# Attention and a feed-forward layer on one core: 20 of 24 joined pairs have their softmax weights turned by VectorE in 32x32 blocks and placed by DMAs through device memory

## The chip, the cores and the metric

The kernel runs on one core of a Trainium2 chip. A core has five engines that run beside one another: TensorE (PE: matmuls; PEld are its weight loads), VectorE (DVE), ScalarE (ACT), GpSimd (POOL) and SyncE (SP), which here only issues DMAs. The metric is the device time of one execution in microseconds (us).

## The reference: what is computed

A batch of 8 with 8 heads, 576 tokens and 64 channels goes through two attentions, whose sum `x` goes through a gated layer of two products:

```python
q_d, k_d, v_d = means of 4 neighbouring tokens        # 144 pooled tokens
out_up    = repeat(softmax(q_d k_d^T / 8) v_d, 4)
out_local = softmax(q k^T / 8 where |i - j| < 4) v     # a band of 7 keys
x   = (out_up + out_local)                             # 4608 tokens x 512 channels
h   = x @ w_in                                         # 2048 hidden channels
out = where(h >= 1, h, where(h <= -1, 0, (h + 1)**2 / 4)) @ w_out
```

## The kernel before

**Two streams on TensorE.** Attention is done a pair of heads at a time; there are 8 x 4 = 32 pairs. The first 8 (`SECOND = 8`) are done in an opening part of their own. The other 24 are done one at a time by the generator `join`, between the steps of the feed-forward layer. The layer is worked through in chunks of 384 tokens; a step `n` is 12 matmuls of the first product (`mm1`, tile `ffn_h`, L858) and 9 of the second (`mm2`, tile `ffn_o`, L921), the second product belonging to an earlier step. `JOINS` lists by hand the steps at which the 24 pairs begin; its last entry is a closing call that only finishes the last pair. `tc.keep_in_program_order` (`put`) fixes the order of all of a join's matmuls on TensorE, so a matmul that waits holds up everything behind it there.

**One join.** The call `join(n)` at step J first issues, on TensorE, the value products of the pair before: `value_ps<-ap,vd` (L633) is the very first of its matmuls, then come the scores of pair n (`score_ps`, L651 and L619) and the local value products `value_ps<-al,v` (L675). During the next step VectorE, GpSimd and ScalarE make the softmax: `sl` holds the local weights (5 pairs of windows of 64 tokens, 128x640), `sp` the pooled ones (128 x 3 x 144). VectorE normalises `sl` at L746 and `sp` at L247 and L254.

**The turn.** The value products need the weights turned, keys on partitions. Before, TensorE does it. For pairs 10 and later (`moved`, 22 of the 24), SP copies `sl` and `sp` to `local` and `pooled` in on-chip memory, which gives the words the type that a one-pass transpose takes (L759, L761, L762). At step J + 2, after that step's `mm2`, TensorE does 5 transposes into `local_ps` (L776) and 6 into `turn_ps` (L779). ScalarE then copies them to `ap` (L784) and `al` (L789), where the next join finds them.

**The DMA queue.** Nearly all DMAs go out from SP in one order; a DMA that waits for its data holds up all that stand behind it. Besides the join's own (`q_sb`, `k_sb`, `v`, `vq_sb` for the next pair) these are the results (`out<-osb`) and sums of weights kept in device memory for the end (`kept<-words`).

Of the kernel before, what the change touches and what calls it, by code (L numbers as in the profile page):

```python
# [10 lines left out]
F32 = mybir.dt.float32  # L11
# [35 lines left out]
WIN = 64  # L47
WIN_START = [0, 58, 116, 174, 232, 285, 343, 401, 459, 512]
OUT_START = [0, 61, 119, 177, 235, 288, 346, 404, 462, 520]
OUT_LEN = [61, 58, 58, 58, 53, 58, 58, 58, 58, 56]  # L50
NB = len(WIN_START)
NG = NB // 2

# [25 lines left out]
QB = 48  # L79
NQB = SD // QB  # L80
# [66 lines left out]
SECOND = 2 * NPAIR  # L147
NALL = B * NPAIR
JOINS = [17, 20, 23, 26, 30, 37, 44, 51, 58, 63, 68, 73, 78, 85, 92, 99, 106, 111, 115, 120, 125]
JOINS += [131, 135, 138, 142]  # L150
assert len(JOINS) == NALL - SECOND + 1


class Rotation:
# [10 lines left out]
def attention_then_ffn(ctx: ExitStack, tc, qT, kT, vw, vp, vq, members, w_in, w_out, out):  # L165
# [431 lines left out]
    def pooled_sums(n):  # L597

        pooled_sum("q")
        pooled_sum("k")  # L600

    def join(n, pool):

        scores = pool.tile([P, 2, 512], F32, name="score_ps", tag="ga")
# [10 lines left out]
        def pooled_scores(i):  # L615
            for h in range(2):
                hs = slice(h * D, (h + 1) * D)
                x = h if i < 2 else 1 - h
                put(nc.tensor.matmul(  # L619
                    sp_v[i][x * D : (x + 1) * D, :],  # L620
                    state["qd"][hs, i * QB : i * QB + D],
                    state["kd"][hs, :],
                    start=True,
                    stop=True,
                    skip_group_check=True,
                ))

        def pooled_values(main):
            ap, vd = state["ap"], state["vd"]
            for h in range(2):  # L630
                hs = slice(h * D, (h + 1) * D)
                ks = slice(0, P) if main else slice((1 - h) * D, (2 - h) * D)
                put(nc.tensor.matmul(  # L633
                    pp_v[hs, :],
                    vd[ks, hs] if main else vd[ks, P : P + D],
                    ap[ks, 0 if main else 1, :, h, :],
                    start=main,
                    stop=not main,
                    skip_group_check=True,
                ))  # L640
# [3 lines left out]
        if n < NALL:  # L644
            q, k = loaded["q"], loaded["k"]
            for g in range(NG):
                for h, s in ((0, 0), (1, 1), (1, 0), (0, 1)):
                    x = h ^ s
                    w = WIN_START[x * NG + g]
                    hs = slice(h * D, (h + 1) * D)  # L650
                    put(nc.tensor.matmul(  # L651
                        sl_v[x * WIN : (x + 1) * WIN, s, g * WIN : (g + 1) * WIN],
                        q[hs, w : w + WIN],
                        k[hs, w : w + WIN],
                        start=True,
                        stop=True,
                        skip_group_check=True,
                    ))
            pooled_scores(0)
        if n > SECOND:  # L660
            pooled_values(False)
        if n < NALL:
            pooled_scores(2)
            pooled_scores(1)
        if n > SECOND:
# [47 lines left out]
        if n > SECOND:  # L713
            x = apool.tile([P, S], F32, name="x", tag="ap", bufs=1)
            xd = apool.tile([P, SD], F32, name="xd", tag="kd", bufs=1)
            nc.vector.tensor_scalar_mul(xd, pp_v, 1.0 / FACTOR)
# [29 lines left out]
        nc.vector.tensor_tensor(  # L746
            slf, slf, scales[:, 0:NB].unsqueeze(2).broadcast_to([P, NB, WIN]), op=ALU.mult
        )
        normalised = normalise(sp, scales)
        vpt = loaded["vp"]  # L750
        vd = apool.tile([P, P + D], F32, name="vd", tag="vd", bufs=1)
        state["vd"] = vd
        with tc.issue_after(shifted.ins):
            nc.gpsimd.tensor_tensor(vpt[:, 0:2, :], vpt[:, 0:2, :], vpt[:, 2:4, :], op=ALU.add)
            nc.gpsimd.tensor_tensor(vd, vpt[:, 0, :], vpt[:, 1, :], op=ALU.add)
        moved = n > SECOND + 1
        if moved:
            local = apool.tile([P, NG * P], F32, name="local", tag="al", bufs=1)
# [559 lines left out]
```

## Time and profile before

| | us |
|---|---|
| median of three runs (lowest to highest) | 889.43 (888.37 to 890.03) |
| the profiled execution: its own time | 889.52 |
| the profiled execution: its span | 887.7 |

| engine | busy us | share of the span |
|---|---|---|
| TensorE matmuls | 876.8 | 99% |
| VectorE | 554.5 | 62% |
| ScalarE | 460.0 | 52% |
| GpSimd | 369.9 | 42% |

The span is what the trace covers, from its first instruction to its last; 1.8 us of the execution's time lie around it. The times in all rows count from the start of the span. The profiled execution stands 0.09 us above the median of the runs. A row of the timeline gives the start, the time that the row covers, the engine, the line, the operation and the tiles; an "x5" merges five neighbouring instructions into one row.

### The profile page before, as it was taken

Reading aid. Unit: us, or ns where it says so; the run is one execution under the profiler, and the core shown is the slowest. Engines: PE = TensorE matmul, PEld = TensorE weight load, DVE = VectorE, ACT = ScalarE, POOL = GpSimd, SP = SyncE. Lnnn points to the kernel's source line nnn. Section 1 sums busy time; section 2 is a strip of 40 time slices with the busy share of each in tenths; the row PEclk is TensorE's granted clock in tenths of the full one; section 3 lists DMA queues with packets and bytes.
Section 4 is the critical chain, followed back from the end, with each engine's and each line's share of the span. In section 5 each row is a group of like instructions: output and inputs, shape, how many; then the busy total and the mean of one; then the engine's idle time right before and its main releaser. Section 6 shows DMA issues by size and latency. Waiting matters only on the chain. (4 is left out here: it accounts for less than half of the span.)

```text
span 887.7 us, 19656 instructions
## 1 busy us (share of the span) xinstructions
PE 876.8 (99%) x7766; PEld 793.7 (89%) x7766; DVE 554.5 (62%) x1062; ACT 460.0 (52%) x1015; POOL 369.9 (42%) x365
## 2 busy tenths in 40 slices
PE   8999999999999999999999999999999999999998
PEld 6788888999999899999999998999999989999997
DVE  7999884775566556566666566665546557744452
ACT  5788864555545545545544544454455544434333
POOL 4366664454334424444433343444334435433232
PEclk9999999999999999999999999999999999999999
DMA  9685113343323423333333233342233222334341
GB/s 351 236 294 198 43 55 126 89 139 106 106 89 103 134 78 106 128 117 116 129 100 106 91 113 99 108 161 93 86 104 99 93 84 75 116 95 143 117 119 51
DMA packets 68172, 106.44 MB, mean 120 GB/s; under 512 B 5712, under 2 KB 34128, under 8 KB 68080
## 3 DMA queue, kind: packets, MB, share of 16 engines
q1 hardware_dynamic: 67648, 104.76, 36.2%
q8 instruction: 61, 1.00, 0.5%
q10 hardware_dynamic: 432, 0.43, 0.1%
q14 instruction: 31, 0.25, 0.1%
HBM read 71.48 MB, written 17.83 MB: 101 GB/s over the span
## 5 line engine op out<-in xcount | busy, mean ns | idle before, releaser
L902 POOL TENSOR_TENSOR gl<-u,gh 128x384 fp32r<-128x384 f32 (+1 forms) x176 | 193.5, 1100 | 395.6 <-ACT gh L896 308.8
L921 PE MATMUL ffn_o<-w_o,gh 128*128 128x512 f32 x1152 | 346.1, 382 | 0.0
L858 PE MATMUL ffn_h<-xh,w_i 128*128 128x384 f32 (+1 forms) x1184 | 301.3, 337 | 0.4 <-ACT m L879 0.2
L921 PEld LDWEIGHTS ffn_o<-w_o,gh 128*128 128x128 f32 x1152 | 211.2, 189 | 24.5 <-issue 0.2
L858 PEld LDWEIGHTS ffn_h<-xh,w_i 128*128 128x128 f32 x1184 | 209.5, 189 | 16.2 <-ACT m L879 4.2
L921 PE MATMUL ffn_o<-w_o,gl 128*128 128x512 f32 x576 | 218.3, 379 | 0.0
L858 PE MATMUL ffn_h<-xl,w_i 128*128 128x384 f32 (+1 forms) x592 | 197.2, 333 | 0.0
L883 DVE TENSOR_SCALAR u<-m 128x384 f32<-128x384 f32 (+1 forms) x160 | 77.4, 483 | 141.2 <-ACT m L879 127.9
L889 DVE SCALAR_TENSOR_TENSOR u<-m,u 128x384 f32<-128x384 f32 (+1 forms) x160 | 107.8, 674 | 79.5 <-ACT u L886 79.5
L896 ACT CAST gh<-u 128x384 fp32r<-128x384 f32 (+1 forms) x176 | 95.5, 542 | 116.2 <-DVE u L889 115.7
L886 ACT ACTIVATE u<-u 128x384 f32<-128x384 f32 (+1 forms) x176 | 97.2, 552 | 111.0 <-DVE u L883 110.6
L921 PEld LDWEIGHTS ffn_o<-w_o,gl 128*128 128x128 f32 x576 | 108.9, 189 | 15.5
L858 PEld LDWEIGHTS ffn_h<-xl,w_i 128*128 128x128 f32 x592 | 111.9, 189 | 2.2
L879 ACT COPY m<-ffn_h 128x384 f32<-128x384 f32 (+1 forms) x132 | 63.8, 484 | 55.8 <-PE ffn_h L858 50.3
L728 ACT ACTIVATE sl<-sl 128x640 f32<-128x640 f32 x24 | 17.8, 740 | 55.5 <-POOL sl L702 55.5
L582 POOL TENSOR_TENSOR xl<-x,xh 128x576 fp32r<-128x576 f32 (+4 forms) x32 | 35.4, 1112 | 16.6 <-ACT xh L581 16.6
L959 DVE SCALAR_TENSOR_TENSOR sums<-sums 128x128 f32<-128x128 f32 (+1 forms) x72 | 33.1, 460 | 1.8
L702 POOL TENSOR_TENSOR sl<-sl,mxl 128x640 f32<-128x640 f32 x24 | 30.3, 1262 | 1.7 <-DVE mxl L701 1.6
L837 POOL TENSOR_TENSOR w_i<-m,w_i 128x512 fp32r<-128x512 f32 x16 | 22.0, 1380 | 21.5 <-ACT w_i L832 21.5
L1078 POOL TENSOR_TENSOR m<-both 128x256 f32<-128x256 f32 x14 | 10.2, 730 | 45.5 <-DVE both L1077 40.9
L837 POOL TENSOR_TENSOR w_o<-m,w_o 128x512 fp32r<-128x512 f32 x16 | 21.8, 1367 | 13.5 <-ACT w_o L832 13.5
L1071 DVE TENSOR_TENSOR both<-ffn_h,both 128x256 f32<-128x256 f32 x14 | 5.9, 424 | 33.9 <-PE ffn_h L1052 29.4
(180 smaller groups left out, 1159.5 us busy)
## 6 DMA issues: line engine op xcount, KB each, us to landing
xh<-kept SPq DMA_DIRECT2D x56, 256.0 KB, 3.7
v<-vw SPq DMA_DIRECT2D x29, 320.0 KB, 4.0
vq_sb<-vq SPq DMA_DIRECT2D x24, 384.0 KB, 3.2
out<-osb SPq DMA_DIRECT2D x35, 256.0 KB, 2.4
raw_o<-w_out SPq DMA_DIRECT2D x16, 512.0 KB, 7.2
raw_i<-w_in SPq DMA_DIRECT2D x16, 512.0 KB, 7.7
kept<-words SPq DMA_DIRECT2D x32, 256.0 KB, 2.6
k_sb<-kT SPq DMA_DIRECT2D x28, 288.0 KB, 4.3
```

What stands on the lines that cost most here:

```text
L582: nc.gpsimd.tensor_tensor(xl[:, p, dst], x[:, part], xh[:, p, dst], op=ALU.subtract)
L702: shifted = nc.gpsimd.tensor_tensor(slf, slf, ml.unsqueeze(2).broadcast_to([P, NB, WIN]), op=ALU.subtract)
L837: engine.tensor_tensor(w[:, 1], raw[name, f, "m"], w[:, 0], op=ALU.subtract)
L858: ins = nc.tensor.matmul(htiles[c, f], wi[:, wt, cc * P : (cc + 1) * P], turns(xt[:, cc, ts]), start=(cc == 0 and xt is xh and wt == 0), s ...
L879: utiles["copied"] = nc.scalar.copy(m, h)
L883: nc.vector.tensor_scalar(utiles[c, f], m if c > 0 else h, -1.0, 1.0, op0=ALU.max, op1=ALU.add)
L886: nc.scalar.activation(u, u, AF.Square, scale=0.5)
L889: utiles["last"] = nc.vector.scalar_tensor_tensor(u, utiles["m"] if c > 0 else h, 1.0, u, op0=ALU.max, op1=ALU.min)
L896: nc.scalar.copy(gh, utiles[c, f])
L902: nc.gpsimd.tensor_tensor(gl, utiles.pop((c, f)), gh, op=ALU.subtract)
L921: ins = nc.tensor.matmul(o, gt[:, ts], turns(weights["o", f][:, wt, :]), start=f == 0 and n == 0, stop=f == NFC - 1 and n == 2,)
L959: return nc.vector.scalar_tensor_tensor(out, a, 1.0, b, op0=ALU.mult, op1=op)
```

## The change

A set `TURNED` holds those pairs, from the third joined pair on, after which at least four steps follow before the next join. By the list `JOINS` these are 20 pairs: 4 of them with four steps to the next join (those that start at steps 26, 111, 131 and 138), 7 with five, 1 with six, 8 with seven. For them:

```diff
+TURN_START = WIN_START[: NG - 1] + [S // 2 - 61] + WIN_START[NG:]
+TURN_PARTS = [[(0, 32, 2)]] + [[(3, 29, 2)]] * (NB - 2) + [[(8, 24, 1), (32, 32, 1)]]
+TURNED = {SECOND + i for i in range(2, NALL - SECOND) if JOINS[i + 1] - JOINS[i] >= 4}
...
+    def turn(n, sl, sp):
+        al = apool.tile([P, NG * P], F32, name="al", tag="al", bufs=1)
+        ap = apool.tile([P, 3, 160], F32, name="ap", tag="ap", bufs=1)
+        nc.vector.transpose(
+            al.rearrange("p (b x c) -> p b x c", b=2, c=32), sl.rearrange("p g r (b c) -> p b (g r) c", c=32)
+        )
+        flat = sl.rearrange("p g r c -> p (g r c)")[:, 0:480].rearrange("p (k i c) -> p k i c", k=5, c=32)
+        nc.vector.transpose(flat[:, 0:4], sp[:, :, 0:P].rearrange("p i (k c) -> p k i c", c=32))
+        nc.vector.transpose(flat[:, 4], sp[:, :, SD - 32 : SD])
+        local = dram.tile([P, NG * P], F32, name="local", tag="local", bufs=2)
+        pooled = dram.tile([160, 2, 160], F32, name="pooled", tag="pooled", bufs=2)
+        for x in range(2):
+            for a in range(2):
+                rows = slice(x * WIN + a * 32, x * WIN + a * 32 + 32)
+                nc.sync.dma_start(
+                    local[x * WIN : (x + 1) * WIN, a * 320 : (a + 1) * 320].rearrange("(b c) f -> c b f", b=2),
+                    al[rows].rearrange("c (b f) -> c b f", b=2),
+                )
+        nc.sync.dma_start(al, local)
+        for x in range(2):
+            for a in range(2):
+                rows = slice(x * WIN + a * 32, x * WIN + a * 32 + 32)
+                nc.sync.dma_start(
+                    pooled[:, x, a * WIN : (a + 1) * WIN].rearrange("(k c) f -> c k f", k=5),
+                    flat[rows, :, 0:2].rearrange("c k i f -> c k (i f)"),
+                )
+            nc.sync.dma_start(
+                pooled[:, 1 - x, P:].rearrange("(k c) f -> c k f", k=5), flat[rows, :, 2],
+            )
+        nc.sync.dma_start(ap[:, 0:2], pooled[0:P])
+        for h in range(2):
+            nc.sync.dma_start(ap[(1 - h) * WIN : (2 - h) * WIN, 2], pooled[160 - WIN : 160, h])
+        state.update(al=al, ap=ap)
...
-                    ap[ks, 0 if main else 1, :, h, :],
+                    ap[ks, h if main else 2, 0:SD] if n - 1 in TURNED else ap[ks, 0 if main else 1, :, h, :],
...
+                    for c0, size, count in TURN_PARTS[i]:
+                        o = TURN_START[i] + c0 - r * S // 2
+                        put(nc.tensor.matmul(
+                            pl_v[hs, r, o : o + size * count],
+                            v[rs, 2 * g + h, :],
+                            turned_part(al, rs, 2 * g + r, c0, size, count),
...
-        normalised = normalise(sp, scales)
+        if n in TURNED:
+            every = scales[:, NB:].unsqueeze(2).broadcast_to([P, NQB, SD])
+            normalised = nc.vector.tensor_tensor(sp, sp, every, op=ALU.mult)
+        else:
+            normalised = normalise(sp, scales)
...
+        if n in TURNED:
+            turn(n, sl, sp)
+            yield
+            load(n + 1, "vp")
...
+            return
```

VectorE turns the 32x32 blocks of `sl` and `sp` where they lie. Four DMAs write the turned local blocks to device memory (`local`) and one reads them back in place (`al`). Six DMAs write the pooled blocks (`pooled`) and three read them back (`ap`). The 11 transposes and the two copies by ScalarE fall away, and with them the three copies by SP. A turned pair's windows are cut a little differently: its local value products are 22 instead of 20, and the scaling of the pooled result (`xd`) is done in two instructions instead of one.

**TensorE, two steps after the join at step 131**, one of the pairs with four steps to the next join. `ffn_o` and `ffn_h` are the second and the first product of the layer. Before:

```order
L921 MATMUL ffn_o_1913<-w_o_752,gl 128x512
L921 MATMUL ffn_o_1921<-w_o_752,gh 128x512 x2
L921 MATMUL ffn_o_1921<-w_o_752,gl 128x512
L776 MATMUL local_ps<-units,local 128x128 x5
L779 MATMUL turn_ps<-units,pooled 128x128 x6
L858 MATMUL ffn_h_1917<-xh,w_i_972 128x384 x2
L858 MATMUL ffn_h_1917<-xl,w_i_972 128x384
```

Now, at the same place:

```order
L1003 MATMUL ffn_o_1913<-w_o_752,gl 128x512
L1003 MATMUL ffn_o_1921<-w_o_752,gh 128x512 x2
L1003 MATMUL ffn_o_1921<-w_o_752,gl 128x512
L940 MATMUL ffn_h_1917<-xh,w_i_972 128x384 x2
L940 MATMUL ffn_h_1917<-xl,w_i_972 128x384
```

The 11 transposes are gone and nothing has come in their place.

**VectorE, the same pair, from the normalising of its weights on.** `u` belongs to the gate of the layer, `first_qd` and `kd` are the pooled sums for the next pair. Before:

```order
L746 TENSOR_TENSOR sl<-sl,score_ps 128x640
L247 TENSOR_TENSOR sp_rest<-sp,score_ps 128x6x16
L254 TENSOR_TENSOR sp<-sp,score_ps 128x3x128
L883 TENSOR_SCALAR u<-m 128x384
L593 TENSOR_REDUCE first_qd<-q_sb 128x144
L889 SCALAR_TENSOR_TENSOR u<-m,u 128x384
L593 TENSOR_REDUCE kd<-k_sb 128x144
```

Now:

```order
L816 TENSOR_TENSOR sl<-sl,score_ps 128x640
L821 TENSOR_TENSOR sp<-sp,score_ps 128x432
L965 TENSOR_SCALAR u<-m 128x384
L616 STREAM_TRANSPOSE al<-sl 128x640
L971 SCALAR_TENSOR_TENSOR u<-m,u 128x384
L620 STREAM_TRANSPOSE sl<-sp 128x384
L621 STREAM_TRANSPOSE sl<-sp 128x96
L598 TENSOR_REDUCE first_qd<-q_sb 128x144
L598 TENSOR_REDUCE kd<-k_sb 128x144
```

The first turn stands behind `u` of a layer step, the other two behind the second half of that gate, and the pooled sums of the next pair behind all three.

**SP's queue, the same pair**, from its own turn to the loads that the next join issues. Before:

```order
L759 DMA local<-sl 128x640
L761 DMA pooled<-sp 128x3x128
L762 DMA pooled<-sp_rest 128x384
L209 DMA vq_sb<-vq 128x768
L203 DMA q_sb<-qT 128x576
```

Now:

```order
L214 DMA vq_sb<-vq 128x768
L627 DMA local<-al 32x2x320 x4
L635 DMA pooled<-sl 32x5x64 x2
L631 DMA al<-local 128x640
L639 DMA pooled<-sl 32x5x32
L635 DMA pooled<-sl 32x5x64 x2
L639 DMA pooled<-sl 32x5x32
L644 DMA ap<-pooled 64x160
L642 DMA ap<-pooled 128x320
L644 DMA ap<-pooled 64x160
L208 DMA q_sb<-qT 128x576
```

Three DMAs have become 14, two of them (`al` and the first `ap`) reading what DMAs of the same pair wrote; the load of `vq_sb` has moved ahead of them.

## Rows read from the trace of the kernel before

**Rows 1.** The page, parts 1 and 2: busy time, and the granted clock in 40 slices.

```profile
PE 876.8 (99%) x7766; PEld 793.7 (89%) x7766; DVE 554.5 (62%) x1062; ACT 460.0 (52%) x1015; POOL 369.9 (42%) x365
...
PEclk9999999999999999999999999999999999999999
```

**Rows 2.** Groups by line and shape, TensorE: count | busy us, mean ns | idle.

```profile
L779 PE MATMUL turn_ps<-units,pooled 128*128 128x128 f32 x132 | 14.9, 250 | 0.0
L776 PE MATMUL local_ps<-units,local 128*128 128x128 f32 x110 | 12.0, 241 | 0.0
```

**Rows 3.** Timeline of TensorE around the transposes of the pair of step 131.

```profile
670.98 0.38 PE L921 MATMUL ffn_o<-w_o,gl 128*128 128x512 f32 x1
671.20 0.55 PE L776 MATMUL local_ps<-units,local 128*128 128x128 f32 x5
671.58 0.68 PE L779 MATMUL turn_ps<-units,pooled 128*128 128x128 f32 x6
672.09 0.56 PE L858 MATMUL ffn_h<-xh,w_i 128*128 128x384 f32 x2
672.49 0.33 PE L858 MATMUL ffn_h<-xl,w_i 128*128 128x384 f32 x1
```

**Rows 4.** Timeline of TensorE at the next join, step 135.

```profile
677.52 0.49 PE L858 MATMUL ffn_h<-xh,w_i 128*128 128x384 f32 x2
677.84 0.33 PE L858 MATMUL ffn_h<-xl,w_i 128*128 128x384 f32 x1
678.10 0.47 PE L633 MATMUL value_ps<-ap,vd 128*64 128x144 f32 x4
...
679.62 0.76 PE L675 MATMUL value_ps<-al,v 64*64 64x61 f32 x40
680.30 0.70 PE L921 MATMUL ffn_o<-w_o,gh 128*128 128x512 f32 x2
```

**Rows 5.** Timeline of VectorE, the pair of step 131.

```profile
666.64 0.82 DVE L746 TENSOR_TENSOR sl<-sl,score_ps 128x640 f32<-128x640 f32 x1
...
667.54 0.55 DVE L254 TENSOR_TENSOR sp<-sp,score_ps 128x384 f32<-128x384 f32 x1
668.01 0.38 DVE L883 TENSOR_SCALAR u<-m 128x384 f32<-128x384 f32 x1
```

**Rows 6.** Timeline of SP's issues, steps 131 to 135.

```profile
667.49 0.51 SPq L759 DMA_DIRECT2D local<-sl  x1
668.23 0.63 SPq L761 DMA_DIRECT2D pooled<-sp  x1
668.90 0.65 SPq L762 DMA_DIRECT2D pooled<-sp_rest  x1
...
679.37 0.33 SPq L203 DMA_DIRECT2D q_sb<-qT  x1
679.81 0.37 SPq L203 DMA_DIRECT2D k_sb<-kT  x1
```

**Rows 7.** DMA issues: count, KB each, median us from issue to landing.

```profile
q_sb<-qT SPq DMA_DIRECT2D x28, 288.0 KB, 3.3
local<-sl SPq DMA_DIRECT2D x22, 320.0 KB, 2.5
pooled<-sp_rest SPq DMA_DIRECT2D x22, 192.0 KB, 2.3
```

**Rows 8.** The line L203 (`q_sb` and `k_sb`, 288 KB each): spread of landing.

```profile
DMA to landing us min/median/max: 2.7/3.7/8.4
```

**Rows 9.** Timelines of VectorE and TensorE, a pair with five steps to the next join.

```profile
595.11 0.55 DVE L254 TENSOR_TENSOR sp<-sp,score_ps 128x384 f32<-128x384 f32 x1
...
609.57 0.47 PE L633 MATMUL value_ps<-ap,vd 128*64 128x144 f32 x4
```

**Rows 10.** Groups by line and shape: one of VectorE, one of ScalarE.

```profile
L889 DVE SCALAR_TENSOR_TENSOR u<-m,u 128x512 f32<-128x512 f32 x32 | 35.9, 1122 | 13.7 <-ACT u L886 13.7
L789 ACT COPY al<-local_ps 128x640 f32<-128x640 f32 x24 | 16.7, 697 | 0.0
```

More of the change, by code (lines that the diff above doesn't have):

```diff
@@ L600, in pooled_sums, with turned_part @@
         pooled_sum("k")
+    def turned_part(al, rows, column, c0, size, count):
+        half = al[rows, (c0 // 32) * 320 + column * 32 + c0 % 32 :]
+        return bass.AP(half.tensor, half.offset, [half.ap[0], (320 - c0 % 32, count), (1, size)])
+    def turn(n, sl, sp):
[31 more added lines that the diff above has]
+        state.update(al=al, ap=ap)
     def join(n, pool):
@@ L618, in pooled_scores @@
                 x = h if i < 2 else 1 - h
+                q0 = min(i * D, SD + D - QB - D) if n in TURNED else i * QB
+                qd = state["qd"][hs, q0 : q0 + D]
                 put(nc.tensor.matmul(
                     sp_v[i][x * D : (x + 1) * D, :],
-                    state["qd"][hs, i * QB : i * QB + D],
+                    qd,
                     state["kd"][hs, :],
@@ L648, in join @@
                     x = h ^ s
-                    w = WIN_START[x * NG + g]
+                    w = TURN_START[s * NG + g] if n in TURNED else WIN_START[x * NG + g]
                     hs = slice(h * D, (h + 1) * D)
@@ L664, in join @@
             pooled_scores(1)
-        if n > SECOND:
+        if n - 1 in TURNED:
+            al, v = state["al"], loaded["v"]
+            for g in range(NG):
+                for r, h in ((0, 0), (1, 0), (0, 1), (1, 1)):
+                    hs = slice(h * D, (h + 1) * D)
+                    s = r ^ h
+                    rs = slice(s * WIN, (s + 1) * WIN)
+                    i = r * NG + g
+                    for c0, size, count in TURN_PARTS[i]:
[4 more added lines that the diff above has]
+                            turned_part(al, rs, 2 * g + r, c0, size, count),
+                            start=r == 0,
+                            stop=True,
+                            skip_group_check=True,
+                        ))
+        elif n > SECOND:
             al, v = state["al"], loaded["v"]
@@ L715, in join @@
             xd = apool.tile([P, SD], F32, name="xd", tag="kd", bufs=1)
-            nc.vector.tensor_scalar_mul(xd, pp_v, 1.0 / FACTOR)
+            if n - 1 in TURNED:
+                there, here = xd[:, 0:P].rearrange("p (i b c) -> p b i c", b=2, i=2), pp_v[:, 0:P]
+                nc.vector.tensor_scalar_mul(there, here.rearrange("p (b i c) -> p b i c", b=2, i=2), 1.0 / FACTOR)
+                nc.vector.tensor_scalar_mul(xd[:, P:], pp_v[:, P:], 1.0 / FACTOR)
+            else:
+                nc.vector.tensor_scalar_mul(xd, pp_v, 1.0 / FACTOR)
             nc.vector.tensor_tensor(
@@ L748, in join @@
         )
-        normalised = normalise(sp, scales)
+        if n in TURNED:
+            every = scales[:, NB:].unsqueeze(2).broadcast_to([P, NQB, SD])
+            normalised = nc.vector.tensor_tensor(sp, sp, every, op=ALU.mult)
+        else:
+            normalised = normalise(sp, scales)
         vpt = loaded["vp"]
@@ L755, in join @@
             nc.gpsimd.tensor_tensor(vd, vpt[:, 0, :], vpt[:, 1, :], op=ALU.add)
+        if n in TURNED:
+            turn(n, sl, sp)
+            yield
+            load(n + 1, "vp")
+            if n + 1 < NALL:
+                with tc.issue_after(normalised.ins):
+                    pooled_sums(n + 1)
+            return
         moved = n > SECOND + 1
@@ L1264, in words, with cut @@
         return np.ascontiguousarray(a).view(np.int64)
-    windows = np.stack([v[:, :, w : w + WIN, :] for w in WIN_START], axis=2)
-    windows = windows.reshape(B, NPAIR, 2, 2, NG, WIN, D).transpose(0, 1, 3, 5, 4, 2, 6).copy()
+    def cut(starts):
+        windows = np.stack([v[:, :, w : w + WIN, :] for w in starts], axis=2)
+        return windows.reshape(B, NPAIR, 2, 2, NG, WIN, D).transpose(0, 1, 3, 5, 4, 2, 6).copy()
+    windows, turned = cut(WIN_START), cut(TURN_START)
     late = windows[SECOND // NPAIR :]
+    for n in TURNED:
+        windows[divmod(n, NPAIR)] = turned[divmod(n, NPAIR)]
     late[..., 1, :] = late[:, :, ::-1, ..., 1, :].copy()
@@ L1281 @@
         blocks[:, :, first : first + SD - P, :, 2] = late[:, :, P:, :, h]
+    for n in TURNED:
+        b, p = divmod(n - SECOND, NPAIR)
+        blocks[b, p, :, :, 2] = np.roll(blocks[b, p, :, :, 2], 3 * (SD - P), axis=0)
     pos = np.arange(WIN)
```

## The prediction

> **What bounds the kernel now.** I began with the page's busy times and its clock line. TensorE's matmuls are busy 99% of the span, VectorE 62%, ScalarE 52%, and the granted clock is full in every slice [rows 1]. So the kernel is as long as TensorE's own instructions, and a change counts by what it takes out of that stream or by the waits that it puts in. Next come the groups by line: 110 + 132 transposes of the copied form are 22 pairs of 5 + 6, 26.9 us of "busy" time [rows 2]. That sum is not yet their price, because neighbouring matmuls overlap. The price is in the timeline of one pair [rows 3]: the transposes start at 671.20, right where a matmul of the layer would have started, and the layer goes on at 672.09. They take 0.89 us of the stream.
>
> The last views show how long the turned weights have until they are needed. For the pair of step 131, VectorE ends the normalising at 667.54 + 0.55 = 668.09 [rows 5], and TensorE comes to the first matmul that reads `ap` at 678.10 [rows 4]: 10.01 us with four steps between the joins. A pair with five steps has 609.57 - 595.66 = 13.91 us [rows 9]. A step is thus worth 3.90 us, and pairs with six or seven have 17.8 and 21.7 us. Before, these times were far from tight. Now two round trips through device memory have to fit.
>
> **What the change removes from TensorE.** The 0.89 us, and a little more: the first two matmuls behind the transposes cover 672.49 - 672.09 = 0.40 us where the usual pair covers 677.84 - 677.52 = 0.32 [rows 3, 4]. I take 0.96 us. The ScalarE copies (0.70 us for `al`, one of two [rows 10]) and SP's three copies go too, but neither engine sets the end.
>
> **What it adds to TensorE.** The local value products are 22 instead of 20 per pair. The 20 take 680.30 - 679.62 = 0.68 us, 0.034 each [rows 4], so two more cost 0.07 us. That their weights are now read as two runs of 29 columns no row shows; the nearest rows are contiguous, I put it at nothing, and with one more such matmul's time per pair at the most (0.03 x 20 = 0.7 us). Net removed: 0.96 - 0.07 = 0.89 us per pair, **17.8 us** for 20. With 0.89 taken as the whole price it would be 16.4.
>
> **What it adds to the way of the weights.** I follow the pair of step 131, with 0 at 668.09, where the normalising ends. (Its pooled half is now one instruction over 432 elements instead of two; the end moves by less than 0.1 us.)
> - The layer's `u` goes first, to 668.01 + 0.38 = +0.30 [rows 5]. The turn of 640 elements is not in the trace; the nearest VectorE instruction over the same 640 is the normalising, 0.82 us [rows 5]. Bounds: not under that, and 640 / 512 x 1.122 = 1.40 us by the slowest shape in the groups [rows 10]. I take 0.82: turned at +1.12.
> - SP issues the first copy 0.03 us after its data is ready (667.46 and 667.49), so at +1.15. Issues that follow each other start 668.90 - 668.23 = 0.67 us apart [rows 6]; one alone takes 0.51. I take 0.67 for a store and 679.81 - 679.37 = 0.44 for a load. The four stores start at +1.15, 1.82, 2.49 and 3.16, two stores of `pooled` at +3.83 and 4.50; the two smaller turns are done by then.
> - Landing: 192 KB took 2.3 us and 320 KB 2.5 [rows 7], 0.2 us for 128 KB. The new stores are of 20 to 80 KB, so 2.1 us; the upper end is 2.5. The last of the four lands at +5.26. Only then can SP issue the load of `al`, and behind it stand the four other stores of `pooled`: +5.70, 6.37, 7.04, 7.71. The last lands at +9.81.
> - Then the loads of `ap`: the first at +9.8, the one that TensorE's first matmul reads at +10.25. The fastest load of 288 KB landed in 2.7 us [rows 8], the median `q_sb` in 3.3 [rows 7]; for 160 KB I take 2.7 - 0.2 = 2.5. **It lands at +12.7.** `al` has landed long before, and the last `ap` is read some 0.5 us later than the first.
>
> **Who waits.** TensorE now comes to the join 0.96 us earlier: at +9.05 with four steps between, at +12.95 with five, later with six or seven.
> - 4 pairs with four steps: 12.7 - 9.05 = 3.65 us each, **14.6 us**. Behind the waiting matmul stand the join and all of the layer, and they are held by order; nothing fills the gap.
> - 7 pairs with five steps: hidden, by 0.25 us. That cover is thin: beyond it each 1 us of delay costs 7 us.
> - 9 pairs with six or seven: hidden by 4 us or more, even with a `kept` store ahead of `ap` in the queue.
> - VectorE's three turns, some 1.6 us per pair (0.82, 0.55 as for its 384 elements [rows 5], and a small one), delay the layer's gates. A gate's result is read two steps (7.8 us) after its product, so I count nothing; without that cover it would be 1.6 x 20 = 32 us. The second instruction for `xd` lies ahead of a VectorE wait for ScalarE: nothing. The 11 more issues on SP hold up `out` and `kept` by a few us, and their buffers come free later: nothing, or up to 1 us in the few pairs that store results there.
>
> **The sum.** 14.6 - 17.8 = -3.2 us. Against the profiled execution's own 889.52 (its span 887.7 and 1.8 around it; 0.09 over the median of the runs) that gives **886.3 us**. It is a difference between two large terms: most of what TensorE gains it would lose again at four joins.
>
> Bounds. With issues 0.51 apart, ten of them save 1.6 us: `ap` lands at +11.1, four waits of 2.05 make 8.2, and the time is 879.9. With stores at 2.5 us (twice 0.4), the load at 3.3 (0.8) and the turn at 1.40 (0.58), it lands at +14.9: 4 x 5.85 + 7 x 1.95 = 37.1, 19.3 us more than before, 908.8. All three together are unlikely.
>
> **Against a rule.** The trace has no such wait of TensorE in the joins, and its clock is full throughout [rows 1]; so no row here shows what the clock does after 3.65 us without a matmul. The Trainium skill, "TensorE: Matmul & The Clock Gate", section "HAM oscillation — how this bites in real kernels", says that waits for DMAs between bursts of matmuls send the clock back to half, each time anew. If it holds here, this is rival 3, whose price comes from rows.
>
> **Rivals.**
> 1. *Short way* (20%). SP issues these small stores faster than the copies of before. `ap` lands at +12 or sooner, by the bound above down to 879.9. For it: a lone issue takes 0.51 and a load 0.33 [rows 6]. Against: the two stores in sequence took 0.63 and 0.65 each.
> 2. *Long way, slower than before* (22%). Issues, semaphores and landings add 1.3 us: `ap` at +14.0. Then 4 x 4.95 + 7 x 1.05 = 27.2 us of waits, 898.9. What decides is the five-step pairs: gain and loss are level at +13.15, and it is slower by more than 0.2% from +13.3. For it: ten issues in a row, each with a wait of its own, and stores of 128 to 256 bytes a piece that no row shows. Against: each step above is taken from a row.
> 3. *The clock falls at the four waits* (9%). The join, 2.20 us at full clock [rows 4], would take twice that at half: 4 x 2.2 = 8.8 us on top, 895.1. For it: the waits are the longest of the whole stream. Against: it takes waits that I only work out, and it is gone where they come out short.
> 4. *The gain isn't there* (4%): other waits of the same joins, such as the scores' wait for `first_qd` and `kd` behind the turns, take the place of the transposes; 889.5. Against: VectorE is done with them by about +3, TensorE asks after +9.
>
> **How the numbers follow.** The forecast, `ap` between +12 and +13.2, has 45%; its own range is 883.5 to 890. About 0.2%, 1.8 us, is what a measurement of this kernel can tell from no change. Faster: 0.34 of the forecast and all of rival 1, 0.54. Same: 0.11 of the forecast, 0.03 of rival 2, 0.01 of rival 3, rival 4: 0.19. Slower: 0.19 of rival 2 and 0.08 of rival 3: 0.27. The range, 879.5 to 897, leaves out half of rival 1's lower tail and the worse half of rival 2, about 0.18.
>
> **What the profile after would show.** No row of `local_ps` and `turn_ps` in 20 pairs, and the layer's products following each other there. TensorE idle ahead of `value_ps<-ap` at the joins of steps 30, 115, 135 and 142, put down to the DMA `ap<-pooled`, some 3.6 us each, and nowhere else. SP: stores 0.67 us apart, the last load of `ap` issued about 10 us after the normalising. I would be wrong if those four waits are under 2 us or over 4.5, if the joins after five steps wait too, if the stores are issued clearly less or more than 0.67 us apart, if the turn takes over 1 us, or if the clock line shows a dip.

## The result and the profile after

The changed kernel takes 894.84 us (median of 5 runs, 893.58 to 895.74), beside 889.73 for the kernel before (5 runs). The ratio is 1.0064, with a 95% interval of 1.0052 to 1.0076: it is slower, by about 5 us. The forecast was 886.3. The profiled execution took 895.74, 6.2 us over that of before, and 894.84 lies in the range of 879.5 to 897.

The page of the kernel after, parts 1 and 2, answers to [rows 1]:

```profile
PE 867.0 (97%) x7626; PEld 784.4 (88%) x7626; DVE 575.2 (64%) x1122; ACT 436.8 (49%) x975; POOL 373.1 (42%) x365
...
PEclk9999999999999999999999999999999999999999
```

TensorE lost 9.8 us of busy time and still the span grew, so it waits now. The clock line looks full as before, because a slice is 22 us long; the drops shown below are too short for it.

The groups of TensorE's matmuls (count | busy us, mean ns | idle ahead of them and what ended it) give the waits by place:

```profile
L940 PE MATMUL ffn_h<-xh,w_i 128*128 128x384 f32 (+1 forms) x1184 | 300.9, 336 | 8.0 <-ACT m L961 8.0
L680 PE MATMUL value_ps<-ap,vd 128*64 128x144 f32 (+1 forms) x192 | 21.6, 301 | 9.8 <-DMA ap<-pooled 6.5 <-DVE u L971 2.2 <-DVE u L965 1.0
```

There are two kinds. 9.8 us are the forecast one, the first value product that waits for `ap`. (3.2 of them are put down to VectorE's `u`, which these products don't read: it ended about when the load landed. At the join of step 30, where this row of the changed kernel names `u`, E6 below names `ap`.) The other 8.0 us were forecast as nothing: the layer's first product waits for ScalarE's copy `m`. Before, the same two places had 0.0 and 0.4 us.

**The forecast wait.** The pair that starts at step 138 has four steps to its join. This is VectorE, SP and TensorE in the timeline (start, us, engine, line, operation; in brackets the idle time and what ended it):

```profile
704.67 0.60 DVE L821 TENSOR_TENSOR sp<-sp,score_ps 128x432 f32<-128x432 f32 x1
...
705.60 0.83 DVE L616 STREAM_TRANSPOSE al<-sl 128x640 f32<-128x640 f32 x1
...
706.46 2.06 SPq L627 DMA_DIRECT2D local<-al  x4
...
708.57 0.93 SPq L635 DMA_DIRECT2D pooled<-sl  x2
...
710.05 0.34 SPq L631 DMA_DIRECT2D al<-local  x1
...
711.86 0.44 SPq L639 DMA_DIRECT2D pooled<-sl  x1
...
714.48 0.51 SPq L642 DMA_DIRECT2D ap<-pooled  x1
...
717.18 0.90 PE L680 MATMUL value_ps<-ap,vd 128*64 128x144 f32 x6 [2.72 <-DMA ap<-pooled]
```

With 0 at the end of the normalising (705.27), the first store goes out at +1.19, the load of `ap` at +9.21, and TensorE goes on at +11.91. The forecast had +1.15, +10.25 and +12.7. Two stores take 0.93 us together, so they are some 0.47 apart and not 0.67; the turn takes 0.83 us (forecast 0.82). The four-step joins wait 2.20 us (step 30), 1.99 (step 135) and 2.72 (step 142). The fourth (step 115) doesn't wait at all, for a reason that follows.

**The wait that was put at nothing.** Another stretch of the same execution, from 364 to 372 us, where a pair's turn falls together with results that go out:

```profile
364.23 0.59 ACT L1027 COPY osb<-ffn_o 128x512 f32<-128x512 f32 x1
...
366.12 0.34 SPq L631 DMA_DIRECT2D al<-local  x1
...
366.98 0.90 SPq L635 DMA_DIRECT2D pooled<-sl  x2
...
367.93 0.44 SPq L639 DMA_DIRECT2D pooled<-sl  x1
...
368.41 1.61 SPq L1028 DMA_DIRECT2D out<-osb  x2
...
371.35 0.48 ACT L961 COPY m<-ffn_h 128x384 f32<-128x384 f32 x1 [3.71 <-DMA out<-osb]
...
371.88 0.59 PE L940 MATMUL ffn_h<-xh,w_i 128*128 128x384 f32 x2 [2.50 <-ACT m L961]
371.91 0.60 SPq L1028 DMA_DIRECT2D out<-osb  x1
```

Read it from the end. TensorE waits 2.50 us for `m`, the copy of its last product out of the bank that it wants to write. `m` waits 3.71 us for a store of `out` to land, because the layer's temporaries rotate through ten buffers and the next one in turn still holds a result. That result, the first of three, was in place at 364.23 + 0.59 = 364.82, but its store went out only at 368.41, right behind the last of the turn's stores. The third store stood behind the loads of `ap` as well, until 371.91. The same at 588.47 holds TensorE for 1.88 us, just ahead of the join of step 115; so TensorE comes to that join at 590.62, by when `ap` has landed (590.29). Two of the rows by engine (what waited, for what: total us, times, longest) show the holders:

```profile
ACT m L961 <- DMA out<-osb: 11.6, 6, 3.7
...
DVE u L965 <- DMA kept<-words: 4.2, 2, 2.2
```

`kept` does harm in a second way. In the pair that starts at step 68, five steps ahead of its join, SP's rows stand in this order:

```profile
396.56 2.27 SPq L1073 DMA_DIRECT2D kept<-words  x2
399.01 0.50 SPq L644 DMA_DIRECT2D ap<-pooled  x1
399.60 0.54 SPq L642 DMA_DIRECT2D ap<-pooled  x1
...
402.72 0.47 PE L680 MATMUL value_ps<-ap,vd 128*64 128x144 f32 x4 [1.04 <-DVE u L965]
```

The load goes out at 11.22 us behind the normalising (which ends at 388.38), and a five-step join waits 1.04 us. Three more, with `kept` ahead of `ap` in the same way, wait 0.79, 0.28 and 0.77 (steps 63, 78 and 111).

**The clock.** Stretches of 4 us behind four of the longest waits (length, then busy us and count of PE, PEld, DVE, ACT and POOL, then the granted clock as a share of 2.4 GHz, the DMA share and GB/s):

```profile
208.00:212.00 4.00, 4.00 (x107) 3.66 (x104) 2.15 (x4) 0.17 (x1) 1.53 (x2) 0.62 0.51 149
...
373.00:377.00 4.00, 4.00 (x14) 3.65 (x14) 1.07 (x3) 1.52 (x3) 1.00 (x1) 0.59 0.18 66
...
683.00:687.00 4.00, 4.00 (x58) 3.72 (x51) 3.60 (x9) 0.95 (x3) 2.27 (x3) 1.00 0.76 230
...
718.00:722.00 4.00, 4.00 (x54) 3.55 (x48) 1.13 (x3) 0.67 (x1) 0.61 (x2) 0.63 0.02 6
```

A mean of 0.6 is a mix of the two levels, 1.2 and 2.4 GHz. So behind the waits of 2.20, 2.50 and 2.72 us the granted clock fell for most of 4 us; behind that of 1.99 it did not.

**The gain** is there as well. Where a five-step pair is turned and nothing waits, the joins stand closer. In the kernel after:

```profile
613.17 0.47 PE L680 MATMUL value_ps<-ap,vd 128*64 128x144 f32 x4
...
614.69 0.89 PE L722 MATMUL value_ps<-al,v 64*64 64x64 f32 x44
615.51 0.70 PE L1003 MATMUL ffn_o<-w_o,gh 128*128 128x512 f32 x2
...
635.17 0.47 PE L680 MATMUL value_ps<-ap,vd 128*64 128x144 f32 x4
```

and in the kernel before, where the same stretch begins at 609.57 [rows 9]:

```profile
632.42 0.47 PE L633 MATMUL value_ps<-ap,vd 128*64 128x144 f32 x4
```

22.85 us became 22.00. The local value products (22, with two records each) take 615.51 - 614.69 = 0.82 us where 0.68 stood before [rows 4].

### The profile page after: what moved, and what is told of

The parts are those of the page before. It is cut to its first block, busy times and chain, and to the rows that moved or that the text cites. A ratio compares the mean times of both kernels' runs of the same rounds, so it can differ in the third digit from the quotient of the medians.

```text
span 893.9 us, 19731 instructions
## 1 busy us (share of the span) xinstructions
PE 867.0 (97%) x7626; PEld 784.4 (88%) x7626; DVE 575.2 (64%) x1122; ACT 436.8 (49%) x975; POOL 373.1 (42%) x365
## 4 chain that ended last, share of the span: by engine, by line
PE 68%; DVE 12%; DMA 7%; ACT 5%; SPq 3%; issue 3%; POOL 1%; DVEq 0%; ACTq 0%; POOLq 0%
PE ffn_o L1003 29%; PE ffn_h L940 22%; PE ffn_h L1134 7%; DVE sums L1041 2%; DMA kept<-words 2%; ACT u L968 2%; ACT sp L800 1%; DMA local<-al 1%; DMA ap<-pooled 1%; PE score_ps L698 1%; DVE u L965 1%; DMA out<-osb 1%; DVE u L971 1%; DMA pooled<-sl 1%; PE value_ps L722 1%
## 5 line engine op out<-in xcount | busy, mean ns | idle before, releaser
L940 PEld LDWEIGHTS ffn_h<-xh,w_i 128*128 128x128 f32 x1184 | 212.0, 190 | 25.3 <-ACT m L961 12.7
L965 DVE TENSOR_SCALAR u<-m 128x384 f32<-128x384 f32 (+1 forms) x160 | 73.3, 458 | 122.3 <-ACT m L961 104.1
L798 ACT ACTIVATE sl<-sl 128x640 f32<-128x640 f32 x24 | 17.8, 740 | 60.8 <-POOL sl L767 45.2
L919 POOL TENSOR_TENSOR w_i<-m,w_i 128x512 fp32r<-128x512 f32 x16 | 25.4, 1596 | 21.5 <-ACT w_i L914 21.5
L680 PE MATMUL value_ps<-ap,vd 128*64 128x144 f32 (+1 forms) x192 | 21.6, 301 | 9.8 <-DMA ap<-pooled 6.5
```

The lines of the kernel that those rows point to most:

```text
L940: ins = nc.tensor.matmul(htiles[c, f], wi[:, wt, cc * P : (cc + 1) * P], turns(xt[:, cc, ts]), start=(cc == 0 and xt is xh and wt == 0), s ...
L965: nc.vector.tensor_scalar(utiles[c, f], m if c > 0 else h, -1.0, 1.0, op0=ALU.max, op1=ALU.add)
```

## The experiments

The theory from the two traces: each turned pair gives TensorE some 0.83 us, and this is more than lost again by (a) waits for `ap` at joins four steps off and at five-step joins with `kept` ahead in the queue, (b) buffers held because `out` and `kept` stand behind the turn in SP's queue, and (c) the clock behind the longest waits. Rivals: the way through device memory is too long in itself; the lower clock is hidden by other work; ScalarE or VectorE is the bound.

All runs (idle us of TensorE by the groups of the profiled execution; m/osb: ahead of `ffn_h` and `ffn_o`; the ratio is to the kernel before on the same chip):

| run | us, median | ratio, 95% interval | idle for ap | for m/osb | mean clock |
|---|---|---|---|---|---|
| changed kernel | 894.84 | 1.0064 [1.0052, 1.0076] | 9.8 | 8.0 | 0.994 |
| E1 five steps and up (16 pairs) | 883.67 | 0.9940 [0.9924, 0.9957] | 2.6 | 5.4 | 0.999 |
| E5 six steps and up (9 pairs) | 885.32 | 0.9954 [0.9941, 0.9967] | 0.0 | 3.7 | 1.0 |
| E3 13 spare products at three joins | 894.83 | 1.0061 [1.0043, 1.0080] | 3.0 | 10.1 | 0.996 |
| E6 8 spare products at three joins | 891.02 | 1.0032 [1.0021, 1.0042] | 3.4 | 7.8 | 0.996 |
| E4 out, kept on ScalarE | 890.83 | 1.0014 [1.0002, 1.0025] | 10.1 | 1.6 | 0.993 |
| E8 out alone on ScalarE | 892.07 | 1.0038 [1.0022, 1.0055] | 12.0 | 2.8 | 0.993 |
| E9 local stores on ScalarE | 883.74 | 0.9942 [0.9929, 0.9954] | 2.0 | 7.8 | 1.0 |
| E10 local, out, kept on ScalarE | 883.85 | 0.9944 [0.9932, 0.9957] | 0.5 | 5.5 | 0.997 |
| E7 16 pairs; out, kept on ScalarE | 878.91 | 0.9888 [0.9874, 0.9901] | 0.3 | 1.2 | 1.0 |
| E12 16 pairs; local, out, kept there | 883.15 | 0.9944 [0.9930, 0.9957] | 0.0 | 3.4 | 0.999 |
| E11 before; out, kept on ScalarE | 889.26 | 1.0013 [1.0005, 1.0022] | 0.0 | 0.0 | 0.999 |
| E13 19 pairs, mixed | 876.64 | 0.9874 [0.9858, 0.9891] | 0.4 | 1.4 | 1.0 |

### E1 and E5: which pairs pay

```diff
-TURNED = {... if JOINS[i + 1] - JOINS[i] >= 4}
+TURNED = {... if JOINS[i + 1] - JOINS[i] >= 5}   # E1; >= 6 in E5
```

Expected of E1:

> Only the 16 pairs with five steps or more are turned by VectorE; the four-step pairs go back to TensorE. Theory A: the loss is made of three things, (a) TensorE's waits for ap, 9.5 us in the profile (6.9 of them after the four-step pairs), (b) the layer's first product waiting for ScalarE's copy of m, 7.5 us, because results and kept sums stand behind the turn's DMAs in SP's queue and hold their buffers, (c) three dips of the granted clock to half, 3.41 us each, 1.7 us lost in each. The four-step waits go (-6.9), the hold-up after step 111 goes (-1.9), two dips go (-3.4), four gains of 0.89 are lost (+3.6): about 886.2. Rival, only the four-step waits count and the clock costs nothing: -6.9 + 3.6, about 891.5. Rival, the waits are filled elsewhere: 894.8 + 3.6 = 898.4.

Expected of E5:

> Only the 9 pairs with six steps or more are turned by VectorE. Theory A: no wait for ap is left, no dip of the clock; of the hold-ups of buffers those in pairs with seven steps stay (0.87, 0.94, 0.59, 0.37, 0.36: 3.1 us); 9 x 0.89 = 8.0 us gained: 889.7 - 8.0 + 3.1, about 884.8. Rival, held buffers cost nothing: 881.7. Rival, the turn itself costs more on TensorE than its transposes did (the strided products): 889.7 or above.

Without the four-step pairs the kernel is 11 us faster than with them, and faster than before. The sum fits without the clock: E5 gives 9 x 0.83 = 7.5, less 3.7 of waits, 3.8; measured 0.46% of 889.2, 4.1 us. E1 gives 16 x 0.83 = 13.3, less 8.0, 5.3; measured 5.3. So the gain per pair is real, and the four pairs cost far more than the 3.3 us that they give: with them go 6.9 us of waits for `ap`, the 1.88 us of (b) ahead of step 115, two drops of the clock and, in E1's trace, the third as well. E1 doesn't tell these apart; E4, E6 and E9 do. That the five-step pairs earn something (E1 against E5) is so by the medians alone: the two intervals overlap. E1 still has 5.4 us of (b).

### E3 and E6: does the clock cost something by itself?

```diff
         if n > SECOND:
+            if n - 1 - SECOND in (3, 21, 23):      # joins at steps 30, 135, 142
+                for _ in range(13):                # E3; range(8) in E6
+                    put(nc.tensor.matmul(values[:, 0, 432:512], ident, ident[:, 0:80], ...))
             pooled_values(True)
```

These are spare products whose results nobody reads; they keep TensorE working in the pause, while the pause's end stays with `ap`. Expected of E3:

> The changed kernel with 13 spare matmuls (80 columns, float32, about 0.13 us each, 1.7 us in all; their result is never read) ahead of the first value product at the three joins where the four-step waits stand (steps 30, 135 and 142). They run while TensorE would wait and wait for nothing themselves. Theory A: two of the three dips of the clock go, 2 x 1.7 us: about 891.4, and the profile keeps one dip, near 373 us. Rival, the dips cost nothing: 894.8; if the spare matmuls are not hidden, up to 3 x 1.7 more, 900.

Expected of E6:

> The changed kernel with 8 spare 80-column products (their results unused) ahead of the first value product at the joins after the pairs of steps 23 (join step 26 on), 138 side: the same three joins as with 13 of them. Measured there, a spare product took 0.22 us, so 8 take 1.76 us, less than the waits of 2.0 to 2.7 us at these joins: the path keeps its end and only TensorE's pause becomes shorter. Theory A (three pauses each cost about 1.7 us more through a granted clock at the lower level for 3.41 us): the two of them that lie at joins vanish, waits for ap there shrink to 0.3 to 0.9 us, and the time is some 3.4 us below the changed kernel's, 891.4 us. Theory B (the lower clock hides behind VectorE and ScalarE and costs nothing by itself): no lower clock at these joins either, and 894.8 us within 0.7.

(The joins meant are those at steps 30, 135 and 142.) E3 missed: a product took 0.22 us and not 0.13, so 13 of them overran the wait and delayed the join; the wait for `m` ahead of step 115 grew as well, to 3.96 us, with a drop of the clock there. E6 is the cleaner test. Its rows at the join of step 30, and the 4 us behind it:

```profile
203.89 1.91 PE L691 MATMUL value_ps<-units 128*128 128x80 f32 x16
206.09 0.47 PE L680 MATMUL value_ps<-ap,vd 128*64 128x144 f32 x4 [0.29 <-DMA ap<-pooled]
```

```profile
208.00:212.00 4.00, 4.00 (x50) 3.72 (x40) 3.60 (x9) 1.10 (x4) 2.32 (x3) 1.00 0.75 228
```

The matmul behind the pause still waits for `ap`, so the path is the same, and the clock stays full here and at step 142. The price of a drop can be read directly: from the join of step 30 to the next the changed kernel takes 31.35 us (its value products start at 207.70 and 239.05), E6 29.79 (206.09 and 235.88), 1.56 us less. From the join of step 142 to the end of the span it is 176.77 against 175.23, 1.54 us. Two other runs repeat the first: the same stretch takes 31.33 us in E4, with a drop there, and 29.79 in E8, without one. Theory B falls.

The whole time is no price, though it came out where theory A put it. It falls by 0.32%, 2.8 us by the ratios, but the profiled E6 has only one drop fewer than the changed kernel: the one near 370 us stays, and ahead of step 115 the wait for `m` is 2.83 us instead of 1.88, now with a drop:

```profile
585.18 1.01 PE L945 MATMUL ffn_h<-xh,w_i 128*128 128x384 f32 x2 [2.83 <-ACT m L966]
```

```profile
584.60:588.10 3.50, 2.92 (x9) 2.92 (x10) 0.92 (x2) 1.51 (x3) 0.73 (x1) 0.51 0.52 166
```

From execution to execution the number differs, too: the mean clock of E6's runs lies between 0.996 and 1.0, that of the changed kernel's between 0.993 and 0.995.

### E4, E8 and E11: who holds the buffers?

```diff
-            nc.sync.dma_start(rows, osb)
+            nc.scalar.dma_start(rows, osb)                  # E4, E8, E11
-            nc.sync.dma_start(kept[f][:, :, t, k], ...)
+            nc.scalar.dma_start(kept[f][:, :, t, k], ...)   # E4, E11
```

E11 is this edit in the kernel before. Expected of E4:

> The changed kernel with the stores of results and of the kept sums issued by ScalarE instead of SP, all 20 pairs turned. Theory A: their buffers are no longer held behind the turn's DMAs (-7.5 us of waits for ScalarE's copy, one dip of the clock less, -1.7), and kept no longer stands ahead of ap in three five-step pairs (-2.6); the four-step waits stay. ScalarE issues 63 stores of about 0.55 us more, at 49% busy. About 883, up to 889 if its issues come in the way of the gates. Rival, the buffers don't matter: 892 (only the 2.6) to 894.8.

Expected of E8:

> Twenty pairs turned; ScalarE issues the stores of out alone, those of kept stay on SyncE's queue. With both on ScalarE it was 890.8 us, with neither 894.8 us. Theory A (out's stores hold the buffers that ScalarE's copy of m waits for, kept's stores delay ap and the u of VectorE): ffn_h waits of the pages' out kind (2.50 and 1.88 us) go, those of kept (0.87, 0.94, 0.59 us) and the waits for ap at steps 63, 73, 111 stay: 890 to 892 us. Theory B (kept's stores are what matters): 894 to 895 us.

Expected of E11:

> The kernel before with one thing changed: ScalarE issues the stores of out and kept. No pair is turned by VectorE. Theory A (these stores cost something only where they stand behind the turn in SyncE's queue; before had 0.2 us of waits for ffn_h in its joined part): no change, 887 to 890 us beside the kernel before at 888 to 889. Theory B (they cost something in themselves, and part of what the versions with stores on ScalarE gained has nothing to do with the turn): 884 to 886 us.

In E4 the waits for `m` fall from 8.0 to 1.4 us, so (b) is shown: nothing changed but whose queue the stores stand in. The time falls by 4 us only, missing the 883 to 889 expected: the join of step 115 is reached earlier and now waits 2.67 us for `ap`, with a clock drop behind it, so that three drops are left as before. E8, with `out` alone, removes the waits of 2.50 and 1.88 us and keeps 0.69 and 0.92; its time of 892.07 is at the edge of theory A's 890 to 892, but the runs scatter from 886.9 to 894.6 and its interval touches E4's, so what `kept` adds to `out` stays unmeasured in time. The scatter goes with the clock: the run at 886.9 us had a mean clock of 0.999, the seven at 892.0 to 894.6 one of 0.991 to 0.993.

In the waits `kept` can be seen: in E8 the five-step joins of steps 63, 73, 78 and 111 wait 0.78, 1.01, 0.35 and 0.86 us, in E4 three of them not at all. The one of step 73 still waits 1.13 us in E4: the load of `ap` goes out at +11.25 there even without `kept` ahead of it, behind a `pooled` store that takes 2.04 us to issue where the others take 0.4 to 0.5; why it does is open. In E7, without such a store, it goes out at +8.47, and nothing waits.

E11 shows no gain of the stores' place in itself: it is 0.13% slower, 1.1 us, and its trace has a wait of 0.63 us near 145 us, ahead of the joined part, that the kernel before has not.

### E9: the length of SP's queue

```diff
             for a in range(2):
-                nc.sync.dma_start(local[...], al[rows]...)
+                nc.scalar.dma_start(local[...], al[rows]...)
```

Expected of E9:

> Twenty pairs turned; the four stores of the local weights to device memory are issued by ScalarE, the rest of the turn stays on SyncE's queue. The queue then issues the pooled weights first: from 1.2 us after the normalising six stores 0.47 us apart end at about 4.0, land some 2.2 to 2.7 us later, and the load of ap goes out at 6.1 to 6.7 instead of 8.0 to 8.8, to land at 8.7 to 9.3 instead of 11.4. Theory A (the loss comes from the length of SyncE's queue, 13 DMAs a pair): the waits for ap at the four-step joins shrink from 2.0 to 2.7 us to 0 to 0.5, the lower clock behind them goes, the stores of out and kept stand 2 us less long behind the turn: 878 to 883 us. Theory B (the loss is the way through device memory itself, the landings in a row, and ScalarE pays for the issues among m, u and gh): 888 to 893 us.

SP's queue now begins with the stores of `pooled`. The pair of step 138 (normalising ends at 696.66):

```profile
698.94 0.81 SPq L635 DMA_DIRECT2D pooled<-sl  x2
...
701.28 0.43 SPq L639 DMA_DIRECT2D pooled<-sl  x1
701.88 0.34 SPq L631 DMA_DIRECT2D al<-local  x1
...
703.06 0.58 SPq L642 DMA_DIRECT2D ap<-pooled  x1
...
706.05 0.74 PE L680 MATMUL value_ps<-ap,vd 128*64 128x144 f32 x6 [0.20 <-DMA ap<-pooled]
```

The load of `ap` goes out at +6.40 instead of +9.21, the wait at this join is 0.20 instead of 2.72, and the clock stays full throughout. With all 20 pairs turned the kernel is 11 us faster than the changed one and faster than before. The way through device memory fits into four steps; what did not fit was the queue. It came out 0.7 us above theory A's range, since 7.8 us of waits for `m` and `osb` remain.

### E7, E10, E12 and E13: together

E7 is E1 with E4's edit, E10 is E9 with it, E12 is E1 with both. E13 turns 19 pairs and gives ScalarE the local stores of three of them:

```diff
-TURNED = {... if JOINS[i + 1] - JOINS[i] >= 4}
+TURNED = {... if JOINS[i + 1] - JOINS[i] >= 4 and i != 17}
...
-                nc.sync.dma_start(local[...], ...)
+                engine = nc.scalar if n - SECOND in (3, 21, 23) else nc.sync
+                engine.dma_start(local[...], ...)
```

with `out` and `kept` on ScalarE everywhere. Expected of E7:

> Two parts at once: only pairs with five or more steps to their join are turned by VectorE (16 pairs), and ScalarE issues the stores of out and kept. Theory A (the loss of the changed kernel is the four-step pairs' wait for ap, the lower clock behind it, and the waits for out and kept buffers that stand behind the turn on SyncE's queue): with sixteen pairs and out, kept on SyncE it was 883.7 us, with 5.4 us of waits for ffn_h and 2.6 us for ap left; without the first, and with ap issued up to 2.5 us earlier in the pairs where kept stood ahead of it, 877 to 880 us. Theory B (what is held up by the queue comes out elsewhere: with the ffn_h waits gone the joins come earlier and wait for ap, as the 2.7 us at the join of step 115 did in the twenty-pair version): 882 to 885 us.

Expected of E10:

> All twenty pairs turned; ScalarE issues the stores of the local weights and those of out and kept, so SyncE's queue holds nine DMAs of a pair's turn and no store of the work between. With the local stores alone on ScalarE it was 883.7 us, with waits of 6.6 us for ffn_h, 1.9 for ap and 1.2 for ffn_o left; sixteen pairs with out and kept on ScalarE took 878.9 us with 1.5 us of waits. Theory A (SyncE's queue is the whole of the loss; each turned pair takes 0.9 us off TensorE): four pairs more than sixteen give 3.6 us, the waits for ap of the four-step joins come to 1 to 2 us: 875 to 878 us. Theory B (ScalarE has no room for 4 to 8 issues more a pair: m and u come later, and the ffn_h waits stay): 880 to 884 us.

Expected of E12:

> Sixteen pairs turned (five or more steps to the join); ScalarE issues the stores of local, out and kept. Without the local ones there it was 878.9 us, with 0.3 us of waits for ap and 1.2 us for ffn_h left. Theory A (a shorter way is worth only the waits that it removes): 878.0 to 879.5 us, no difference beyond the waits. Theory B (SyncE's queue still delays loads or stores without a wait that the trace names, or ScalarE pays for 64 more issues): more than 1 us away on one side or the other.

Expected of E13:

> Nineteen pairs turned: all with five or more steps to their join and three of the four four-step ones (joins at steps 30, 135 and 142; not the one at 115). ScalarE issues the stores of out and kept everywhere, and those of the local weights in the three four-step pairs only. Theory A (the sixteen-pair version with out and kept on ScalarE, 878.9 us, lost nothing at these joins, and in the twenty-pair version with the same stores on ScalarE the stretches that end at the joins of steps 30, 135 and 142 were 0.71, 0.83 and 0.61 us shorter than in it, while the one that ends at step 115's was 2.1 longer): 878.9 - 2.15 = 876.8 us, in 876 to 877.5. Theory B (the issues of the local stores on ScalarE take from the work between the joins what the turn gives, as they did by 3.4 us ahead of the join of step 68): 878.5 to 881 us.

E7 is where theory A put it: 878.91. Its waits are nearly gone:

```profile
L940 PE MATMUL ffn_h<-xh,w_i 128*128 128x384 f32 (+1 forms) x1184 | 300.7, 336 | 1.2 <-ACT m L961 1.2
...
L680 PE MATMUL value_ps<-ap,vd 128*64 128x144 f32 (+1 forms) x192 | 21.3, 298 | 0.3 <-DMA ap<-pooled 0.3
```

E10 (883.85, theory B) and E12 (883.15, far from theory A) show a new loss. E12 differs from E7 only in who issues the local stores, and is 4.2 us slower by the medians (5.0 by the ratios). Join by join the two go side by side except in one stretch, from step 63 to 68, which takes 25.47 us instead of 22.06. ScalarE there (ACTq: DMAs that it issues):

```profile
360.05 0.83 ACTq L627 DMA_DIRECT2D local<-al  x2
...
362.25 0.52 ACT L968 ACTIVATE u<-u 128x384 f32<-128x384 f32 x1 [1.32 <-DVE u L965]
362.26 0.31 ACTq L627 DMA_DIRECT2D local<-al  x1
...
363.82 1.07 ACT L1027 COPY osb<-ffn_o 128x512 f32<-128x512 f32 x2
364.43 1.25 ACTq L1028 DMA_DIRECT2D out<-osb  x2
365.72 0.59 ACT L1027 COPY osb<-ffn_o 128x512 f32<-128x512 f32 x1 [0.83 <-ACT osb L1027]
...
368.26 0.48 ACT L961 COPY m<-ffn_h 128x384 f32<-128x384 f32 x1 [1.96 <-DMA out<-osb]
```

The copies of `osb` stand behind the local stores in ScalarE's order, the last of these behind a `u` that waits 1.32 us for VectorE; so the results' stores go out later, and `m` waits for them again. In E7 the first of these copies starts at 360.43. The queue's length was moved to ScalarE, and the same buffers are held from there. E13 avoids this by putting the local stores on ScalarE only where four steps are to be met: 876.64, in the 876 to 877.5 expected, 1.26% below the kernel before (0.9874, 0.9858 to 0.9891). It and E7 are the fastest, with 19 and 16 pairs turned by VectorE and the stores of results issued by ScalarE: so neither of these engines' own work was the bound in the changed kernel.

## Why the prediction was wrong

**The step that failed** is the last of those put at nothing: "The 11 more issues on SP hold up `out` and `kept` by a few us, and their buffers come free later: nothing, or up to 1 us in the few pairs that store results there." It measured 8.0 us of waits for `m` (0.4 before), and a clock drop behind the longest. I had priced the stores by whether TensorE reads them, which it doesn't; but ScalarE and VectorE need their buffers back, and TensorE needs ScalarE's copy within a step. E4 shows the cause: the same stores from another queue bring it to 1.4.

**The four-step wait** had the right mechanism and the wrong size: 3.65 us each, measured 2.20, 1.99 and 2.72, and none at step 115; 6.9 instead of 14.6. The term that was too large is the store's 0.67 us in the queue, measured 0.47: in the pair of step 138 the last store goes out at +6.59 and not +7.71. Rival 1's short way came true, by 0.8 us, and did not bring its result.

**The five-step pairs** were hidden by 0.25 us by my count. Three of seven are hidden. The other four wait 0.79, 1.04, 0.28 and 0.77 us, 2.9 in all, with `kept` ahead of `ap` in the queue (E4 and E7 take these waits away, but for the one at step 73 in E4 and 0.34 us at step 63 in E7): I had allowed for that store in the pairs with six and seven steps, and not here.

**The clock** was rival 3, with 9% and 8.8 us. It came, at two of the four-step waits and at one of the waits for `m`. The price per drop was 1.54 to 1.56 us (E6) and not 2.2: a mean of 0.62 over 4 us leaves out 1.5 us of full-speed work. Three make 4.7 us. I gave it too small a chance because I held it for gone where the waits came out short; 2.2 us were enough. The Trainium skill, "TensorE: Matmul & The Clock Gate", section "HAM oscillation — how this bites in real kernels", says that DMA waits between bursts of matmuls send the clock back each time; the trace agrees in kind, with drops behind waits for `ap` of 2.20 and 2.72 us, but not each time: none behind 1.99.

**The gain** of 0.89 us per pair measured 0.82 to 0.85 in stretches without a wait. The two runs of 29 columns, which no row showed, are the likely rest: the local products take 0.14 us more and not 0.07. Over 20 pairs it is 16.6 us, not 17.8.

**What held:** the turn's 0.83 us; the gates' slack (VectorE's 1.6 us per pair left E7, with 16 pairs turned, no more than 1.2 us of waits for `m`); and no new wait of the scores (rival 4).

**Its own signs.** Of the signs of being wrong that it names, three came: a four-step wait under 2 us (1.99, and none at step 115), waits after five steps, and stores clearly closer than 0.67 us; the clock dropped as well, too briefly for the clock line. That 894.84 lies in the stated range all the same is luck: 7.7 us too much at the four joins stand against 7.6 us of held buffers, 4.7 of the clock and 2.9 at five-step joins that the sum left out.

The sum by its own terms: -16.6 + 9.8 + (8.0 - 0.4) + 3 x 1.56 = +5.5 us, where the profiled executions differ by 6.2 and the medians by 5.1. In E9 it doesn't close as well: 16.6 - 2.0 - 7.8 is 6.8 us, and 0.58% is 5.2; in E13 19 x 0.83 - 1.8 is 14.0, and 1.26% is 11.2. Two things are in that gap. All runs with `out` on ScalarE, E13 too, have the 0.63 us near 145 us that E11 shows. And the idle time of the rows, which begins at the end that the profile gives for the matmul before, can be less than a wait costs: in E13 the stretches from the joins of steps 37 and 44 hold the same matmuls and take 29.81 and 30.69 us, with 0.26 us idle in the second. How much of the rest this makes up is open.

What the runs found is in the Trainium skill, too: "Perfetto Trace Analysis", section "DMA Optimizations", says that balancing DMAs over the engines that can issue them may help where generating their descriptors is the bottleneck, and that giving inputs and outputs an issuing engine each may make sense. E7 (against E1) and E9 (against the changed kernel) agree, with 4.6 and 10.8 us by the ratios; E12 is the counterexample, 4.2 us slower than E7 where the second engine had its own work behind the issues.

## What to carry to other kernels

Where a queue is in order, price a new DMA by everything that comes to stand behind it, and ask of each of those whose buffer it frees: a result that nobody on the critical path reads can still hold the bank that TensorE writes next. A move that is worth 0.8 us where it is hidden can cost several where it is not; so choose it place by place, by the slack of each (16 pairs of 20 already turn the sign). And when a queue is too long, move the part that the waiting chain passes first, and only onto an engine with nothing due behind it.

## What was not expected of the hardware

- TensorE's clock fell behind pauses much shorter than I had reckoned with, and not by length alone. In the changed kernel, E4 and E8 it fell behind waits of 2.20, 2.50 and 2.72; 2.05, 2.67 and 2.10; 2.35, 2.18 and 2.08 us. It did not behind 1.99 (changed kernel), 2.13 (E4) and 2.32 (E8). What tells those apart is open; the same kernel doesn't always have the same number of drops, by the mean clocks of its runs (E4: 0.989 to 0.998, with 892.91 and 888.02 us).
- In E10 it fell behind three waits close together, of 0.80, 0.37 and 1.23 us within 4.1 us. In E12 the waits at the same place are 0.80, 0.34 and 1.52 us, and the clock stayed full.
- Small stores issued one behind the other started 0.47 us apart here, against 0.67 for the larger ones of before [rows 6].
- With most moving operands read as two runs of 29 columns, 22 local products took 0.82 us, 0.037 each; 20 with one run took 0.68, 0.034 each [rows 4].
